# The first stage of a long convolution's transform, moved from the attention loop into the projection phase

## The chip, the cores and the metric

The kernel runs on one core of one Trainium2 chip, in one launch. A core has a matrix engine (PE, with its weight loads shown apart as PEld), a vector engine (DVE), an activation engine (ACT), a general engine (POOL) and a queue that issues the DMAs of this kernel (SP). The metric is the device time of one execution in microseconds; a kernel's time is the median of its runs.

## The reference: a state-space convolution beside multi-head attention

The output holds two results side by side, each 2048 rows of 448 columns. The left half is a long convolution of `u` with a kernel `K` that is a sum of 256 damped oscillations per column, done in the frequency domain at twice the length:

```python
def _A_ref(u, log_A_real, A_imag, C_real, C_imag, log_dt, D_skip):
    L = u.shape[1]
    dt = jnp.exp(log_dt)
    A = -jnp.exp(log_A_real) + 1j * A_imag
    C = (C_real + 1j * C_imag) * dt[:, None]
    P = jnp.exp((A * dt[:, None])[:, :, None] * pos[None, None, :])
    K = 2.0 * jnp.einsum("dn,dnl->dl", C, P).real
    Kf = jnp.fft.rfft(K, 2 * L)
    Uf = jnp.fft.rfft(u_t, 2 * L)
    y = jnp.fft.irfft(Uf * Kf[None, :, :], 2 * L)[:, :, :L]
    return y + u * D_skip[None, None, :]
```

The right half is softmax attention over 16 heads of 28 columns: `x @ wqkv`, scores times `28 ** -0.5`, softmax, times `v`, and the output projection `wo`. All numbers are float32.

## The kernel before, in words

**Projection phase.** The code from line 212 to line 551 computes q, k and v and the seeds of the convolution kernel. `work` (line 495) lists 48 projections (`qk_proj`, `v_proj`: twelve matmuls each) in four blocks of 512 rows of x; `transposes` (line 438) brings each block of x into the needed layout through the two PSUM banks `pt` (pool `ps_t`). Beside them run eight blocks of `seeds` (line 313), thirteen stages each, on DVE, ACT and POOL, which build the powers that the loop multiplies up. Both are laid out on 41 slots (line 530): in slot t the projections up to a share (t+1)/37 of the work are written, then the seed stages of that slot (stage i of block o in slot 4o + i, its load two slots ahead), then what `ahead[t]` holds, which are loads for the loop (from slot 26 on). In this phase instructions are not kept in the order in which they are written: a planner at build time orders them for each engine by its own estimates. The order on each engine and on SP's queue is then fixed. After slot 37 the tiles for the first units of attention are loaded (`khat`, `qhat`, `v`), and the maxima of unit 0 are computed.

**Attention loop.** From line 1006 a loop of 256 steps, written out, runs over 16 units (4 groups of heads by 4 blocks of queries) of 16 blocks of 128 keys. A step computes four score products `pss`, four products `pm` for the maxima of a later unit, four exponentials on ACT, and the eight passes of `po` that apply `p` to `v`. Here the order is that of the program on all engines (`KEPT["a"]`). Each step has two places `f` at which `slot` (line 957) puts one piece of side work: the building of the convolution kernel (`m_due`, 56 blocks, one every 3.5 steps, with its powers on DVE and POOL), then pieces of the transform of u (`u_due`), and late in the loop the spectrum and the final stage of the convolution.

**The transform of u** has two stages. The 2048 rows are seen as 32 by 64 (row = 64 n1 + n2). Stage 1 (`u_stage1`, line 567) takes, for four values of n2 in each of 16 rounds, sums over n1 with cosines and sines (`w1`, a block matrix of four 32 by 32 blocks); a round has one load step of four DMAs (each 32 partitions, rows of 112 elements), two parts (cosine, sine: one PSUM tile, four strips of matmul, one ACT copy into `ub`), and four DMAs that store to `yu_d`. Stage 2 (`u_stage2`, line 589) reads `yu_d` again, for two values of k1 in each of 16 rounds, with a matrix `mt` of its own (`m2u`), and leaves `uh_d` for the spectrum.

`u_due` (line 894) gives the step of each part: round i, part c at 3 + 3i + 1.5c, and 4 steps later for the rounds of stage 2, so that stage 1 runs over the steps 3 to 50 and stage 2 over the steps 55 to 104. The load of a round stands two rounds ahead. After the last part `load_wo` (line 704) clears and loads the output weights into the `ua` buffers of the same pool.

Of the kernel before, what the change touches and what calls it, by code (L numbers as in the profile page):

```python
# [8 lines left out]
F32 = mybir.dt.float32  # L9
F32R = mybir.dt.float32r  # L10
I32 = mybir.dt.int32
AF = mybir.ActivationFunctionType
# [6 lines left out]
D = 448  # L19
# [4 lines left out]
HG = H // G  # L24
CQ = 512
NQ = L // CQ
NK = L // 128
# [12 lines left out]
UG = (2, 2, 4)  # L40
PS = 1
SGB, XB, XL = 2, 5, 4
K0, KP, KD, UP = 0, 3.5, 4, 3
A0, A1, KW = 26, 34, (33, 35, 36)

N1 = 32
N2 = 64
CI = D // 4
# [42 lines left out]
def body(ctx, tc, a, out):  # L91
    nc = Engines(tc)
    nc.kept = KEPT["p"]
    x, wqkv, wo, u_a = a["B_x"][0], a["B_wqkv"], a["B_wo"], a["A_u"][0]
    out = out[0]
# [7 lines left out]
    dram = ctx.enter_context(tc.tile_pool(name="dram", bufs=1, space=DRAM))  # L103
# [1 line left out]
    kd_d = [dram.tile([2, 128, CQ], F32, name=f"kd_{g}") for g in range(G)]  # L105
    q_d = [[dram.tile([2, 128, CQ], F32, name=f"q_{g}_{c}") for c in range(NQ)] for g in range(G)]
    sd_d = [dram.tile([BO, 128, SDF], F32, name=f"sd_{o}") for o in range(NO)]
    yu_d = dram.tile([128, N1, D], F32, name="yu_d")
    uh_d = [dram.tile([128, N1 // 2, 2, DF], F32, name=f"uh_{f}") for f in range(2)]
    yk_d = [dram.tile([128, N1 // 4, NBF, 32], F32, name=f"yk_{f}") for f in range(2)]  # L110
    v_d = [dram.tile([128, G, NK // NQ, HG * 32], F32, name=f"v_{c}") for c in range(NQ)]
# [3 lines left out]
    const = pool(ctx, "const")  # L115
# [2 lines left out]
    sel = const.tile([128, HG], F32, name="sel")  # L118
    kones = const.tile([128, 1], F32, name="kones")
    w1 = const.tile([128, 2, 128], F32, name="w1")  # L120

    att, k0_st = ExitStack(), ExitStack()
    ps_w, n_ring = [None, 3], [0]

    def w_tile():

        n_ring[0] += 1
        return ps_w[0].tile([128, CQ], F32, name=f"pm{n_ring[0] % ps_w[1]}")

    q_p = pool(att, "q_p", side="right")  # L130
    v_p = pool(att, "v_p", side="right")
    kd_p = pool(att, "kd_p", side="right")
# [3 lines left out]
    def mm32(o, w, x_, start, stop, at=0):  # L136

        for i in range(w.shape[-1] // 32):
            c = slice(32 * i, 32 * i + 32)
            nc.tensor.matmul(o[c], w[:, c], x_, start=start, stop=stop, tile_position=(0, at + 32 * i))  # L140
# [4 lines left out]
    def load_k(g, j, p):  # L145
        if j == 0:
            t = k0_t if g == 0 else p.tile([128, HG, L], F32R, name="khat")
            kt_g[g] = [t[:, i] for i in range(HG)]
        for r in range(4):
            nc.sync.dma_start(kt_g[g][j][32 * r:32 * r + 32, :].bitcast(F32), k_d[g][r % 2, 32 * j:32 * j + 32, :])  # L150
# [61 lines left out]
    with ExitStack() as st:  # L212
# [6 lines left out]
        ps_t = pool(st, "ps_t", 2, PSUM)  # L219
# [40 lines left out]
        t = a["A_log_dt"]  # L260
# [7 lines left out]
        nc.gpsimd.memset(half_pi, TWO_PI / 4)  # L268
        nc.sync.dma_start(sel, a["sel"])
        nc.sync.dma_start(w1, a["w1"])  # L270
        for k in range(NCK):
            for s in (1, 0):
                src = wns[k][:, s, :].rearrange("p (g h e) -> p g h e", g=G, e=DH)
                hi, lo = (w_g[:, i, s, k, :, :, :DH] for i in range(2))
                nc.scalar.activation(hi, src, AF.Copy)
                nc.vector.tensor_tensor(lo, src, hi.bitcast(F32), ALU.subtract)
            nc.scalar.activation(vh[:, k, :], wns[k][:, 2, :], AF.Copy)
            nc.gpsimd.tensor_tensor(vl[:, k, :], wns[k][:, 2, :], vh[:, k, :].bitcast(F32), ALU.subtract)
# [201 lines left out]
        def v_proj(c, t):  # L480
# [11 lines left out]
                nc.sync.dma_start(v_d[c][:, :, t], vs.rearrange("p (g h) e -> p g (h e)", g=G))  # L492
            return evac

        work = []
        for c in range(NQ):
            jobs = [lambda c=c, s=s, g=g: qk_proj(c, s, g) for g in range(G) for s in (1, 0)]
# [15 lines left out]
        ahead = collections.defaultdict(list)  # L513
# [4 lines left out]

        for j, t in enumerate(KW):
            ahead[t].append(lambda j=j: load_k(0, j, k0_p))  # L520

        def project():

# [31 lines left out]
    kq_p = pool(kq_st, "kq_p")  # L555
# [8 lines left out]

    late = [False]

    def u_stage1(q):
        t_ = {}

        def load():  # L570
            u_in = t_["in"] = kq_p.tile([128, 8, CI], F32, name="ua", bufs=2)[:, :4]
            for j in range(4):
                nc.sync.dma_start(u_in[32 * j:32 * j + 32], bass.AP(
                    tensor=u_a.tensor, offset=u_a.offset + 4 * q * D + j * CI, ap=[[N2 * D, 32], [D, 4], [1, CI]]))

        def part(c):
            if c == 0:
                t_["out"] = kq_p.tile([128, 2, 4, CI], F32, name="ub", bufs=2)
            u_in, yt = t_["in"], t_["out"]
            pw = w_tile()  # L580
            mm32(pw[:, :D], w1[:, c, :], u_in.rearrange("p n i -> p (n i)"), start=True, stop=True)
            nc.scalar.activation(yt[:, c].rearrange("p n i -> p (n i)"), pw[:, :D], AF.Copy)
            if c == 1:
                for j in range(4):
                    nc.sync.dma_start(yu_d[8 * q:8 * q + 8, :, j * CI:(j + 1) * CI].rearrange("r k i -> k r i"),
                                      yt[32 * j:32 * j + 32].rearrange("p c n i -> p (c n) i"))
        return [load, lambda: part(0), lambda: part(1)]

    def u_stage2(m):
        t_ = {}  # L590

        def load():
            yu = kq_p.tile([128, 2, D], F32, name="ua", bufs=2)
            mt = kq_p.tile([128, 2, 128], F32, name="mt", bufs=2)
            t_["in"] = yu, mt
            nc.sync.dma_start(yu, yu_d[:, 2 * m:2 * m + 2, :])
            nc.sync.dma_start(mt, a["m2u"][:, 2 * m:2 * m + 2, :])

        def part(c):
            if c == 0:  # L600
                t_["out"] = kq_p.tile([128, 2, 2, DF], F32, name="ub", bufs=2)
            (yu, mt), us = t_["in"], t_["out"]
            pw = w_tile()
            for e in range(2):
                mm32(pw[64 * e:64 * e + 64, :D], mt[:, e, 64 * c:64 * c + 64], yu[:, e, :], True, True, 64 * e)
            for f in range(2):
                nc.scalar.activation(us[:, f, c, :].rearrange("p (b j i) -> p j b i", j=4, i=2),
                                     pw[:, f * DF:(f + 1) * DF].rearrange("p (j b i) -> p j b i", j=4, i=2), AF.Copy)
            if c == 1:
                for f in range(2):  # L610
                    nc.sync.dma_start(uh_d[f][:, m], us[:, f])
        return [load, lambda: part(0), lambda: part(1)]
# [260 lines left out]
    urgent, back = collections.deque(), collections.deque()  # L873
    powers = {"g": collections.deque(), "e": collections.deque()}
    done = {"mm": -1}
    u_jobs = [u_stage1(q) for q in range(16)] + [u_stage2(m) for m in range(16)]

    def u_load(i):
        if i < 32:
            u_jobs[i][0]()  # L880

    def u_part(i, c):
        u_jobs[i][1 + c]()
        if c and i not in (14, 15):
            u_load(i + 2)
        if c and i == 15:
            u_load(16)
            u_load(17)
        if c and i == 31:
            load_wo()  # L890

    u_load(0)
    u_load(1)
    u_due = collections.deque((3 + UP * i + (UP / 2) * c + (4 if i > 15 else 0), i, c) for i in range(32) for c in range(2))
    k_due = collections.deque(range(NB))
    m_due = collections.deque()

# [177 lines left out]
def constants():  # L1075
    import numpy as np
    k = {}
    k["ident"] = np.eye(128)
    sel, ones = np.zeros((128, HG)), np.zeros((128, 1))
    for j in range(HG):  # L1080
        sel[32 * j + DH, j] = 1.0
        ones[32 * j + DH:32 * j + DH + 2] = 1.0
    k["sel"], k["kones"] = sel, ones
    k["pw2"] = np.tile(2.0 ** np.arange(LV), (128, 1))
    n1, k1 = np.arange(N1), np.arange(N1)
    n2, k2 = np.arange(N2), np.arange(N2)
    th = 2 * np.pi * np.outer(n1, k1 + 0.25) / N1
    w1 = np.zeros((2, 128, 128))
    wb = np.zeros((2, 2, N1, 2, N1))
    for j in range(4):  # L1090
        w1[0, 32 * j:32 * j + 32, 32 * j:32 * j + 32] = np.cos(th)
        w1[1, 32 * j:32 * j + 32, 32 * j:32 * j + 32] = np.sin(th)
    for h in range(2):
        wb[h, 0, :, h, :] = np.cos(th).T / L
        wb[h, 1, :, h, :] = np.sin(th).T / L
    k["w1"] = w1.transpose(1, 0, 2)
    k["wb"] = wb.transpose(0, 1, 2, 4, 3).reshape(128, N2)
    ph = 2 * np.pi * ((k1[:, None, None] + 0.25) * n2[None, :, None] / L + n2[None, :, None] * k2[None, None, :] / N2)
    c, s = np.cos(ph).transpose(1, 0, 2), np.sin(ph).transpose(1, 0, 2)
    m2 = np.zeros((2, N2, N1, 2, 64))  # L1100
    m2[0, :, :, 0], m2[0, :, :, 1] = c, s
    m2[1, :, :, 0], m2[1, :, :, 1] = -s, c
    k["m2u"] = m2.reshape(2, 16, 4, N1, 128).transpose(1, 0, 2, 3, 4).reshape(128, N1, 128)
    wa = np.zeros((2, 64, N1, N2, 2))
    ct, st = c.transpose(2, 1, 0), s.transpose(2, 1, 0)
    wa[0, ..., 0], wa[0, ..., 1] = ct, -st
    wa[1, ..., 0], wa[1, ..., 1] = st, ct

    wa = wa.reshape(2, 64, N1, 2, 2, 16, 2).transpose(0, 1, 2, 5, 4, 3, 6)
    k["mw"] = np.concatenate([m2.reshape(128, N1, 128), wa.reshape(128, N1, 128)], -1)  # L1110
    return {n: v.astype(np.float32) for n, v in k.items()}
# [18 lines left out]
```

## Time and profile before

| | |
|---|---|
| median of three runs | 1304.48 us (1301.89 to 1305.05) |
| span of the profiled execution, first to last instruction | 1301.1 us |
| total of the profiled execution beyond its span | not given |
| instructions | 33177 |
| mean granted clock of PE | 0.978 |
| DMA moved | 205.35 MB, mean 158 GB/s |

The prediction sets its sum against the span and says how it stands to the median. In the rows, a group is named by engine, operation, output and input tiles; "x32" is the number of instructions. In the view by stretches, the columns are the stretch and its length, then busy time and instructions of each engine, then the clock that PE was granted, the busy share of the 16 DMA engines and what they moved. All instructions stand under line 75, a helper through which every operation goes; so they are told apart by the names of tiles.

### The profile page before, as it was taken

What the parts mean: (1) busy time and instruction counts of PE and PEld (TensorE: products, weight loads), DVE (VectorE), ACT (ScalarE), POOL (GpSimd) and SP (SyncE); (2) the same over time, 40 slices, a digit from 0 to 9 for tenths busy, and PEclk for the clock granted to TensorE, in tenths of its full rate; (3) what the DMA queues carried; (4) which work ended last, traced back from release to release, by engine and by line L of the source; (5) the groups of instructions that cost most, each with busy time, mean ns of one, the idle gap of its engine ahead of it and who ended that gap; (6) DMA issues with size and microseconds to landing.
All of it is one profiled execution on the core that took longest, in us unless ns stands there. A gap on an engine that the chain in (4) does not pass through costs nothing.

```text
span 1301.1 us, 33177 instructions
## 1 busy us (share of the span) xinstructions
PE 1228.2 (94%) x12625; PEld 701.0 (54%) x12625; DVE 948.0 (73%) x2106; ACT 952.4 (73%) x2068; POOL 871.1 (67%) x736
## 2 busy tenths in 40 slices
PE   6878985899999999999999999999999999999997
PEld 5657763355555555555555555555555555544433
DVE  5887896987777887787788888888888655645111
ACT  4775763488888888888888888888887766756552
POOL 3676683298888878888869999998996212424421
PEclk9888997999999999999999999999999999999999
DMA  6677769835866555458644131733425453647656
GB/s 194 203 258 244 249 206 294 237 77 124 195 137 149 124 146 148 140 147 231 181 126 96 54 95 32 182 91 83 103 51 148 153 158 133 201 144 244 198 162 174
DMA packets 200088, 205.35 MB, mean 158 GB/s; under 512 B 95993, under 2 KB 158521, under 8 KB 197881
## 3 DMA queue, kind: packets, MB, share of 16 engines
q1 hardware_dynamic: 199928, 203.23, 56.2%
q8 instruction: 100, 1.64, 0.5%
q14 instruction: 60, 0.48, 0.1%
HBM read 120.73 MB, written 82.18 MB: 156 GB/s over the span
## 4 chain that ended last, share of the span: by engine, by line
PE 71%; DVE 10%; DMA 6%; POOL 5%; ACT 3%; issue 3%; SPq 0%; POOLq 0%; ACTq 0%; DVEq 0%
PE pm L75 40%; PE pss L75 16%; PE po L75 15%; DVE tri L75 2%; DVE mx L75 2%; POOL e L75 1%; POOL qhat L75 1%; DMA k<-hl 1%; ACT tri L75 1%; DVE qhat L75 1%; DVE sg L75 1%; DMA tri<-in_B_wqkv 1%; DVE px L75 1%; DMA khat<-k 1%; DMA ut<-in_A_u 1%
## 5 line engine op out<-in xcount | busy, mean ns | idle before, releaser
L75 ACT ACTIVATE p<-pss 128x512 f32<-128x512 f32 x1024 | 560.9, 609 | 111.6 <-PE pss L75 108.6
L75 PE MATMUL pss<-qhat,khat 128*128 128x512 f32 x1024 | 402.5, 399 | 1.5 <-ACT p L75 1.4
L75 DVE TENSOR_REDUCE mx<-pm 128x1 f32<-128x512 f32 x500 | 321.4, 684 | 109.2 <-PE pm L75 107.1
L75 PE MATMUL pm<-khat,qhat 128*128 128x512 f32 x749 | 326.3, 438 | 3.4 <-DVE mx L75 2.1
L75 POOL TENSOR_TENSOR e<-e,sdb 128x256 f32<-128x256 f32 x168 | 202.0, 1202 | 116.2 <-ACT e L75 61.2
L75 PE MATMUL po<-p,v 128*32 128x512 f32 x2048 | 269.1, 594 | 0.0
L75 POOL TENSOR_TENSOR e<-e,eu 128x256 f32<-128x256 f32 x168 | 248.4, 1478 | 13.2
L75 PEld LDWEIGHTS pm<-khat,qhat 128*128 128x128 f32 x749 | 141.0, 189 | 199.7 <-ACT p L75 47.8
L75 DVE CUSTOM_DVE_ANT_0 rl<-pm,rl 128x512 f32<-128x512 f32 x249 | 171.4, 688 | 65.2 <-ACT rl L75 61.5
L75 PEld LDWEIGHTS pss<-qhat,khat 128*128 128x128 f32 x1024 | 190.2, 188 | 45.7 <-issue 10.8
L75 POOL TENSOR_TENSOR eu<-e,sdb 128x256 f32<-128x256 f32 x168 | 202.2, 1203 | 0.0
L75 POOL TENSOR_TENSOR p<-pr,pr 64x448 f32<-64x448 f32 x64 | 73.3, 1145 | 158.5 <-PE pm L75 133.2
L75 ACT ACTIVATE rl<-pm 128x512 f32<-128x512 f32 x249 | 150.8, 606 | 20.4 <-PE pm L75 20.4
L75 DVE TENSOR_TENSOR g<-g,zg 128x128 f32<-128x128 f32 x392 | 162.1, 413 | 3.4
L75 PE MATMUL pm<-xh,khat 112*128 112x512 f32 x256 | 94.1, 451 | 23.2 <-DVE hl L75 11.1
L75 PE MATMUL pm<-kdif,qhat 128*128 128x512 f32 x249 | 100.5, 404 | 2.6 <-DMA v<-v 1.3
L75 DVE TENSOR_TENSOR zg<-g,zg 128x128 f32<-128x128 f32 x224 | 88.0, 393 | 5.0
L75 PEld LDWEIGHTS pm<-e,g 128*32 128x32 f32 x3584 | 57.2, 109 | 43.8 <-issue 16.1
L75 DVE TENSOR_TENSOR pr<-pm,ub 128x448 f32<-128x448 f32 x64 | 37.0, 619 | 56.4 <-PE pm L75 42.0
L75 PEld LDWEIGHTS pm<-xh,khat 112*128 112x128 f32 x256 | 54.2, 217 | 39.4 <-DVE hl L75 12.9
L75 PE MATMUL pm<-e,g 128*32 128x64 f32 x3584 | 73.0, 222 | 1.9 <-POOL e L75 1.9
L75 ACT ACTIVATE y<-pm 128x448 f32<-128x448 f32 x48 | 26.5, 553 | 58.2 <-PE pm L75 33.8
(134 smaller groups left out, 1470.3 us busy)
## 6 DMA issues: line engine op xcount, KB each, us to landing
sdb<-sd SPq DMA_DIRECT2D x56, 336.0 KB
khat<-k SPq DMA_DIRECT2D x64, 256.0 KB
qhat<-q SPq DMA_DIRECT2D x64, 256.0 KB
sd<-sg SPq DMA_DIRECT2D x8, 1456.0 KB
k<-hl SPq DMA_DIRECT2D x16, 512.0 KB
q<-hl SPq DMA_DIRECT2D x16, 512.0 KB
mw<-in_mw SPq DMA_DIRECT2D x16, 512.0 KB
sd<-qhat SPq DMA_DIRECT2D x8, 896.0 KB
```

Source lines behind the costliest of these rows:

```text
L75: i = f(*args, **kw)
```

## The change

Stage 1 leaves the loop. Its 16 rounds stand in the slots `U1` of the projection phase, the load one slot ahead of the two parts. A round now takes the rows q, q + 16, q + 32, ... of u (128 of them, one on each partition, in full rows of 448), by one DMA; the block matrix is reordered to that (`wu`, a constant of its own beside `w1`, which other code still uses). Each part stores its 128 rows by one DMA. The tiles are borrowed: the input from the `v` buffers, the output from the `kdif` tiles, PSUM from `pt`. `yu_d` and the rows of `m2u` are reordered; stage 2 reads its input by two DMAs of 64 partitions in place of one. In the loop, `u_due` holds stage 2 alone, one round every 6 steps (`UP`) in place of 3, from step 3 on.

```diff
-K0, KP, KD, UP = 0, 3.5, 4, 3
+K0, KP, KD, UP = 0, 3.5, 4, 6
 A0, A1, KW = 26, 34, (33, 35, 36)
+U1 = (3, 4, 5, 6, 7, 8, 11, 12, 13, 14, 16, 17, 20, 21, 22, 23)
...
-    yu_d = dram.tile([128, N1, D], F32, name="yu_d")
+    yu_d = dram.tile([16, 4, N1, 2, D], F32, name="yu_d")
...
+    wu = const.tile([128, 2, 128], F32, name="wu")
...
+        nc.sync.dma_start(wu, a["wu"])
...
+        def u_stage1(q):
+            t_ = {}
+
+            def load():
+                t_["in"] = v_p.tile([128, NK // NQ, HG, 32], F32, name="v", bufs=5).rearrange("p t h e -> p (t h e)")[:, :D]
+                nc.sync.dma_start(t_["in"], u_a.rearrange("(p q) d -> q p d", q=16)[q])
+
+            def part(c):
+                ps = ps_t.tile([128, CQ], F32, name="pt")[:, :D]
+                mm32(ps, wu[:, c, :], t_["in"], True, True)
+                yt = kd_p.tile([128, CQ], F32R, name=f"kdif{2 * (q % 2) + c}").bitcast(F32)[:, :D]
+                nc.scalar.activation(yt, ps, AF.Copy)
+                nc.sync.dma_start(yu_d[q].rearrange("s k c d -> c (s k) d")[c], yt)
+            return load, lambda: part(0), lambda: part(1)
...
+        for q, t in enumerate(U1):
+            load, cos, sin = u_stage1(q)
+            ahead[t - 1].append(load)
+            ahead[t] += [cos, sin]
...
-    def u_stage1(q):
-        t_ = {}
-
-        def load():
-            u_in = t_["in"] = kq_p.tile([128, 8, CI], F32, name="ua", bufs=2)[:, :4]
-            for j in range(4):
-                nc.sync.dma_start(u_in[32 * j:32 * j + 32], bass.AP(
-                    tensor=u_a.tensor, offset=u_a.offset + 4 * q * D + j * CI, ap=[[N2 * D, 32], [D, 4], [1, CI]]))
-
-        def part(c):
-            if c == 0:
-                t_["out"] = kq_p.tile([128, 2, 4, CI], F32, name="ub", bufs=2)
-            u_in, yt = t_["in"], t_["out"]
-            pw = w_tile()
-            mm32(pw[:, :D], w1[:, c, :], u_in.rearrange("p n i -> p (n i)"), start=True, stop=True)
-            nc.scalar.activation(yt[:, c].rearrange("p n i -> p (n i)"), pw[:, :D], AF.Copy)
-            if c == 1:
-                for j in range(4):
-                    nc.sync.dma_start(yu_d[8 * q:8 * q + 8, :, j * CI:(j + 1) * CI].rearrange("r k i -> k r i"),
-                                      yt[32 * j:32 * j + 32].rearrange("p c n i -> p (c n) i"))
-        return [load, lambda: part(0), lambda: part(1)]
...
-            nc.sync.dma_start(yu, yu_d[:, 2 * m:2 * m + 2, :])
+            for c in range(2):
+                nc.sync.dma_start(yu[64 * c:64 * c + 64], yu_d.rearrange("q s k c d -> c (q s) k d")[c, :, 2 * m:2 * m + 2])
...
-    u_jobs = [u_stage1(q) for q in range(16)] + [u_stage2(m) for m in range(16)]
+    u_jobs = [u_stage2(m) for m in range(16)]
...
-        if c and i not in (14, 15):
+        if c:
             u_load(i + 2)
         if c and i == 15:
-            u_load(16)
-            u_load(17)
-        if c and i == 31:
             load_wo()
...
-    u_due = collections.deque((3 + UP * i + (UP / 2) * c + (4 if i > 15 else 0), i, c) for i in range(32) for c in range(2))
+    u_due = collections.deque((3 + UP * i + (UP / 2) * c, i, c) for i in range(16) for c in range(2))
...
+    wu = np.zeros((N1, 4, 2, 4, N1))
+    for j in range(4):
+        wu[:, j, 0, j], wu[:, j, 1, j] = np.cos(th), np.sin(th)
+    k["wu"] = wu.reshape(128, 2, 128)
...
-    k["m2u"] = m2.reshape(2, 16, 4, N1, 128).transpose(1, 0, 2, 3, 4).reshape(128, N1, 128)
+    k["m2u"] = m2.reshape(2, 4, 16, N1, 128).transpose(0, 2, 1, 3, 4).reshape(128, N1, 128)
```

More of the change, by code (lines that the diff above doesn't have):

```diff
@@ L875, in body @@
     done = {"mm": -1}
-    u_jobs = [u_stage1(q) for q in range(16)] + [u_stage2(m) for m in range(16)]
+    u_jobs = [u_stage2(m) for m in range(16)]
     def u_load(i):
-        if i < 32:
+        if i < 16:
             u_jobs[i][0]()
```

## The prediction, made before the changed kernel ran

> **What bounds the kernel now.** I read the page first: busy time, the 40 slices, the shares of the chain that ended last.
>
> ```profile
> PE 1228.2 (94%) x12625; PEld 701.0 (54%) x12625; DVE 948.0 (73%) x2106; ACT 952.4 (73%) x2068; POOL 871.1 (67%) x736
> ...
> PE   6878985899999999999999999999999999999997
> ...
> PEclk9888997999999999999999999999999999999999
> DMA  6677769835866555458644131733425453647656
> ...
> PE 71%; DVE 10%; DMA 6%; POOL 5%; ACT 3%; issue 3%; SPq 0%; POOLq 0%; ACTq 0%; DVEq 0%
> ```
>
> There are two regimes. For the first eight slices (about 254 us, the projection and the loads at its end) PE has gaps and a granted clock below full; from then on PE is at 9. The change takes work out of the second regime and puts it into the first, so I asked for busy times by stretch, and for the chain before 254 us alone.
>
> ```profile
> core 0: us, PE busy (x) PEld busy (x) DVE busy (x) ACT busy (x) POOL busy (x), PEclk, DMA share, GB/s
> 25.00:133.00 108.00, 88.50 (x386) 70.69 (x385) 88.22 (x155) 76.18 (x153) 69.67 (x77) 0.89 0.70 238
> 133.00:206.00 73.00, 60.27 (x263) 48.47 (x261) 59.74 (x101) 49.72 (x98) 55.36 (x61) 0.91 0.71 226
> 206.00:254.00 48.00, 32.27 (x78) 15.78 (x79) 39.15 (x87) 13.41 (x26) 2.43 (x4) 0.82 0.95 278
> 264.00:461.00 197.00, 196.42 (x2339) 107.28 (x2331) 154.07 (x365) 163.24 (x366) 163.33 (x129) 1.00 0.59 133
> 472.00:665.00 193.00, 192.07 (x2295) 104.68 (x2284) 149.60 (x354) 161.83 (x390) 151.17 (x119) 1.00 0.61 163
> 700.00:800.00 100.00, 99.73 (x1225) 57.22 (x1217) 87.45 (x208) 85.30 (x194) 96.63 (x79) 1.00 0.32 77
> ```
>
> ```profile
> by line: DVE tri L75 10.7%; PE pm L75 8.3%; POOL qhat L75 6.8%; DMA k<-hl 6.2%; issue 5.8%; ACT tri L75 5.1%; DVE qhat L75 5.0%; DVE sg L75 4.9%; DMA tri<-in_B_wqkv 4.2%; DVE px L75 4.2%; DMA khat<-k 3.9%; POOL tri L75 3.5%; DVE hl L75 3.1%
> ```
>
> In the loop PE is busy for 196.42 of 197 us: what leaves PE there shortens the run. Before it no engine rules: the chain hops between DVE, PE, POOL, ACT and DMA, the largest entry 10.7%, and each is 65 to 82% busy in 25 to 133 us. That is the dangerous kind of place: nothing is full, so added work is neither free nor fully paid.
>
> **What the loop gives back.** A part of stage 1 is one `u_stage1` call of `part(c)`: eight matmul passes and one ACT copy; there are 32, two in every three steps. Busy times of pipelined matmuls overlap, so I price a part by the pace of the steps. `fin` copies `po` once in 16 steps:
>
> ```profile
> 316.69 0.60 ACT L75 ACTIVATE o<-po 128x512 f32<-128x512 f32 x1
> 446.39 0.71 ACT L75 ACTIVATE o<-po 128x512 f32<-128x512 f32 x1
> ...
> 757.65 0.60 ACT L75 ACTIVATE o<-po 128x512 f32<-128x512 f32 x1
> ...
> 986.01 0.71 ACT L75 ACTIVATE o<-po 128x512 f32<-128x512 f32 x1
> ```
>
> The first pair is 32 steps with stage 1: 129.70/32 = 4.053 us. The second is 64 steps without any u: 228.36/64 = 3.568 us. The difference, 0.485 us a step, is 0.728 us a part (1.5 steps), against a mean of 0.94 us busy (30.1/32 from the row below). Stage 2 keeps its 32 parts, one every 3 steps instead of two: about 3.568 + 0.243 = 3.81 us a step up to step 99. So the loop gives 32 x 0.728 = **23.3 us**. The busy sum would say 30.1, but its excess is drain under the next matmul.
>
> Could another engine set the floor first? POOL is the next: 96.63 us in 100 us at the 3.568 us pace is 3.45 us a step, below 3.81. ACT and DVE have more room. The stall at the end of stage 2 stays: `load_wo` still clears two `ua` tiles on POOL behind the last stage-2 part.
>
> ```profile
> 664.24 0.85 POOL L75 MEMSET ua<- 128x896 f32 x1 [11.14 <-PE pm L75]
> ...
> PE pm L75 <- POOL e L75: 1.9, 2, 1.3
> ```
>
> POOL's 11.14 us there cost PE 1.9 us, in the chain; I keep that as it is (its change is worth 2 us either way at most).
>
> **What is moved to the projection.**
>
> ```profile
> L75 PE MATMUL pm<-ua,w 128*32 128x448 f32 x256 | 30.1, 541 | 0.0
> L75 ACT ACTIVATE ub<-pm 128x448 f32<-128x448 f32 x32 | 17.6, 550 | 19.6 <-PE pm L75 18.7 <-ACT ub L75 0.7
> ...
> L75 SPq DMA_DIRECT2D ua<-in_A_u x64: 311/430/1812, 250.6 to 434.3; - x64
> ...
> L75 SPq DMA_DIRECT2D yu_d<-ub x64: 302/450/1663, 273.8 to 461.1; - x64
> ...
> yu_d<-ub SPq DMA_DIRECT2D x64, 112.0 KB
> ...
> ua<-in_A_u SPq DMA_DIRECT2D x64, 56.0 KB
> ...
> L75 POOL TENSOR_TENSOR tri<-tr,pw x8: 2244/2249/3445, 31.1 to 181.4; 128x1232 f32<-128x1232 f32 x8
> ```
>
> The rounds stand in slots 3 to 23. The last row dates them: `phases` of seed block o stands in slot 4o + 4, so seven blocks, 28 slots, take 150.3 us, 5.37 us a slot; slot 3 is at about 26 us and the end of slot 23 near 138 us. The stretch of 25 to 133 us is theirs.
>
> *PE* gets the same 32 parts (the block matrix `wu` has the shape of `w1`), 23.3 us at full clock, on 88.50 busy of 108; idle are 19.5 there and 12.7 up to 206 us, 32.2 in all. *ACT* gets 17.6 us, 76.18 to 93.8 of 108. *DMA* gets (56 + 112) KB x 64 = 11.0 MB. At the 238 GB/s that 0.70 of the engines moved here (340 at a share of 1) that is 32 us of full DMA, 0.30 of the stretch: 0.70 becomes 1.00. In the loop the same bytes cost nothing, under a PE that is full at a share of 0.59. *SP* issues 16 loads and 32 stores and one constant (0.43 to 0.45 us each, about 22 us) and is spared 128 issues in the loop, where it gains 16 for the second halves of the stage-2 loads; those lie two rounds, 12 steps, ahead. The constant is 128 KB once. *Buffers*: the rounds borrow the `v` and `kdif` tiles, whose own loads come after slot 25; PSUM comes from the two `pt` banks that the transposes of x use.
>
> The DMA term can also be read by row length. 264 to 461 us, where these stores go out in rows of 448 B, gives 133/0.59 = 225 GB/s at a share of 1; the changed rows have 1792 B, like the longer rows of the projection at 340. The Trainium skill ("DMA: Bandwidth & Descriptors", section Specifications) asks for at least 512 B for full rate; these two rows agree. At 225 the 11.0 MB would be 49 us and the case below would lose 17 us more; at 340 it is the 32 us that I use.
>
> How much of this lengthens the projection? Waits of this stretch (PE's and ACT's, then the DMA queue's own):
>
> ```profile
> PE pm L75 <- DVE kb L75: 6.8, 4, 4.3
> PE pm L75 <- DVE hl L75: 6.8, 2, 5.4
> ...
> PE pt L75 <- DVE xl L75: 5.7, 3, 2.8
> ...
> ACT hl L75 <- DMA k<-hl: 3.2, 2, 2.3
> ACT vst L75 <- DMA v<-vst: 3.2, 2, 2.2
> ```
>
> ```profile
> SPq L75 <- POOL dhl L75: 33.9, 8, 8.4
> SPq L75 <- DVE hl L75: 13.5, 5, 4.9
> ```
>
> PE's gaps, 19.3 of 19.5 us, are waits for DVE to empty PSUM, in pieces of up to 5.4 us: an independent part placed there is free, one placed elsewhere pushes the next projection by 0.73 us. The order on PE is fixed at build time, so it can't choose at run time. From below the lengthening is -2 us: a warm PE can give back some of its 0.11 of lost clock on its 8.3% of 254 us of chain. From above it is 32 us, the DMA time with nothing hidden under it, the largest of the added loads. I take **12 us**, half of the PE time: PE would be asked for 88.50 x 0.89 + 23.3 = 102 of 108 us at full clock, too close to full for all to hide, while the gaps and the stretch up to 206 us hold more than 23.3. What is late next is the chain of seeds on ACT, through 32 copies of 0.55 us queued ahead of its own, then the loads before the loop.
>
> **Sum.** 1301.1 - 23.3 + 12 = 1289.8 us of span. The runs' median is 3.4 us over that profile's span (the profiled execution's own total isn't given; the fastest run lies 0.8 over it), so 1293 us. The bounds give 1301.1 + 3.4 - 23.3 - 2 = 1279 and 1304.5 - 23.3 + 32 = 1313.
>
> **Rivals.**
>
> *All of it hides, and the clock pays.* After an idle gap PE is slow:
>
> ```profile
> 83.00 2.08 PE L75 MATMUL pm<-xh,khat 112*128 112x512 f32 x4 [5.38 <-DVE hl L75]
> 84.87 0.63 PE L75 MATMUL pm<-xl,khat 112*128 112x512 f32 x1
> ...
> 89.89 0.63 PE L75 MATMUL pm<-xh,khat 112*128 112x512 f32 x2
> 90.36 0.40 PE L75 MATMUL pm<-xl,khat 112*128 112x512 f32 x1
> ```
>
> Four matmuls take 1.87 us from start to start (0.47 each) behind a gap of 5.38 us, and two 0.47 (0.235 each) some 5 us later. At a clock of 0.89 the 88.50 busy us hold 9.7 lost ones. u parts in the gaps would keep PE at 0.235; then the lengthening is 0 or a little less: 1281 us. For it: the idle 32.2 us exceed 23.3. Against it: the gaps of the waits above are few (nine), the parts 32. The Trainium skill ("TensorE: Matmul & The Clock Gate", Part 1) has the clock halve after an idle window of about 3.4 us; the rows above agree, and by that rule a part in each long gap speeds up what follows.
>
> *The projection takes it all back.* If the parts land between projections and not in gaps, each costs its 0.73 us again: 23.3 back, 1304 us. For it: the static order, and two `pt` banks that now serve parts and transposes in turn.
>
> *Slower: the DMA engines fill up.* Place: slots 3 to 23. The shares add to 1.00; the stretch from 206 us shows a share of 0.95, with PE busy for only 32.27 of 48 us. SP issues in order and stands up to 8.4 us for one `dhl`; a load of u queued there comes late, PE stands before its part, and `hl`, `vst` and `dhl`, with few buffers, stay taken by slow stores (the 3.2 us waits above grow). Price: up to the 32 us of DMA, less 23.3: +8.7, 1313 us. It decides once the stretch's share passes about 0.95 and its length 108 + 23 us. Against it: rounds leave out five of the 21 slots, and 133 to 206 us at 0.71 can take bytes that are late.
>
> *Not what it says*: the loop could keep its pace, if the 0.485 us a step came from ACT's or SP's share and not from PE. PE's 196.42 of 197 speaks against it; I give it no chance of its own.
>
> **How the numbers follow.** Half hidden (1285 to 1300) 0.45; all hidden 0.22; all taken back 0.17; DMA-bound 0.16. A measurement of this kernel can tell about 0.3%, 3.9 us, from no change, so the first two are faster (0.67), the third the same, the fourth slower. The range takes the bounds, 1279 to 1313.
>
> **What would show it.** The loop begins with the first `pss`:
>
> ```profile
> L75 PE MATMUL pss<-qhat,khat x1024: 387/396/505, 254.0 to 1275.7; 128*128 128x512 f32 x171
> ```
>
> Right: steps 16 to 48 of the loop at about 3.81 us (was 4.05) and a loop 23 us shorter from the first `pss` on; the first `pss`, now at 254.0 us, near 266; the stretch of 25 to 133 us stretched by some 10 us with PE's clock at or above 0.89 and a DMA share of 0.85 to 0.95. Wrong: a first `pss` after 277 us (taken back or worse; then the waits say whether for DMA or for PE), a step above 3.9 us (the pace wasn't PE's), or a gap in front of the u matmuls that a load ends.

## The result, and the profile after

Before: 1303.18 us median of 4 runs (1300.64 to 1305.05). After: 1309.63 us (1309.46 to 1311.34, 4 runs). The ratio is 1.0052, with a 95% interval of 1.0037 to 1.0067: half a per cent slower, where 1293 us had been forecast. The profiled execution of the changed kernel has a span of 1309.2 us (before 1301.1).

The first question is which half of the sum failed. Three groups of the changed kernel, by tile; the columns are the count, the shortest, median and longest duration in ns, then the first and last start in us:

```profile
L76 PE MATMUL pss<-qhat,khat x1024: 387/396/595, 284.4 to 1283.6; 128*128 128x512 f32 x171
...
L76 POOL TENSOR_TENSOR tri<-tr,pw x8: 2242/2248/2754, 31.5 to 204.0; 128x1232 f32<-128x1232 f32 x8
...
L76 ACT ACTIVATE hl<-pm x16: 577/594/637, 22.2 to 239.5; 128x512 fp32r<-128x512 f32 x16
```

The last of these groups in the kernel before:

```profile
L75 ACT ACTIVATE hl<-pm x16: 571/592/629, 21.8 to 210.1; 128x512 fp32r<-128x512 f32 x16
```

The loop begins at 284.4 us, **30.4 later** than before (254.0). From there to the end of the span it takes 1309.2 - 284.4 = 1024.8 us, **22.3 less** than before (1301.1 - 254.0 = 1047.1). The balance is the 8.1 us between the spans. The delay is there by the last copy of a projection (`hl<-pm`: 210.1 to 239.5, +29.4), and the stretch from it to the first `pss` is as long as it was (43.9 and 44.9 us). So it arose where the rounds were put; the seeds' `tri` lost 22.6 us of it (181.4 to 204.0).

The pace of the steps, by the copies that end steps 16, 32 and 64 of the changed kernel's loop (start, duration):

```profile
344.20 0.60 ACT L76 ACTIVATE o<-po 128x512 f32<-128x512 f32 x1
...
405.24 0.60 ACT L76 ACTIVATE o<-po 128x512 f32<-128x512 f32 x1 [0.17 <-PE po L76]
...
526.93 0.60 ACT L76 ACTIVATE o<-po 128x512 f32<-128x512 f32 x1 [0.16 <-PE po L76]
```

61.04/16 = 3.815 and 121.69/32 = 3.803 us a step, against a forecast of 3.81.

Now the projection. Busy times by stretch, from 25 us to the point some 4 us before the last `hl` copy, first in the kernel before, then in the changed one (columns as in the prediction):

```profile
25.00:206.10 181.10, 148.77 (x648) 119.16 (x646) 148.06 (x255) 125.90 (x249) 125.13 (x137) 0.90 0.70 233
```

```profile
25.00:235.40 210.40, 178.14 (x906) 123.75 (x904) 146.31 (x255) 143.75 (x283) 122.21 (x137) 0.92 0.76 253
```

PE is idle for 181.1 - 148.8 = 32.3 us of the first and for 210.4 - 178.1 = 32.3 us of the second. Its idle time, which was to take up half of the added matmuls, is as long as before; so PE's busy time and the stretch grew alike, by 29.4 and 29.3 us. What PE waits for (in total, times, longest), before and then after; `hl`, `kb`, `xl` and `vst` are tiles into which DVE or ACT copy results out of PSUM, `kdif` is the borrowed output tile:

```profile
PE pm L75 <- DVE hl L75: 13.2, 6, 5.4
PE pm L75 <- DVE kb L75: 6.8, 4, 4.3
PE pt L75 <- DVE xl L75: 6.1, 4, 2.8
```

```profile
PE pm L76 <- DVE kb L76: 8.2, 3, 5.1
PE pm L76 <- DVE hl L76: 7.3, 4, 3.9
PE pt L76 <- ACT kdif L76: 6.5, 3, 3.3
PE pt L76 <- DMA v<-in_A_u: 4.4, 1, 4.4
PE pt L76 <- DVE xl L76: 1.5, 2, 1.2
```

The waits for DVE did shrink, from 26.1 to 17.0 us. In their place stand two that the moved work brought with it: for the ACT copies of its own parts (6.5) and for a load of u (4.4). And parts do not stand only in gaps. The timeline of PE in the changed kernel, where two rounds run back to back with projections:

```profile
157.21 0.63 PE L76 MATMUL pm<-xh,khat 112*128 112x512 f32 x2
157.68 0.40 PE L76 MATMUL pm<-xl,khat 112*128 112x512 f32 x1
158.00 1.71 PE L76 MATMUL pt<-v,wu 128*32 128x448 f32 x16
159.64 0.73 PE L76 MATMUL pm<-xh,khat 112*128 112x512 f32 x2
...
162.31 0.40 PE L76 MATMUL pm<-xl,khat 112*128 112x512 f32 x1
162.64 1.71 PE L76 MATMUL pt<-v,wu 128*32 128x448 f32 x16
164.28 0.73 PE L76 MATMUL pm<-xh,khat 112*128 112x512 f32 x2
```

Sixteen matmuls, two parts, push the next projection by 1.64 us (158.00 to 159.64): 0.82 a part, against the 0.728 that a part cost in the loop. There nothing is hidden.

### The profile page after: what moved, and what is told of

Its sections match the earlier page's. It is cut to its first block, busy times and chain, and to the rows that moved or that the text cites. A ratio compares the mean times of both kernels' runs of the same rounds, so it can differ in the third digit from the quotient of the medians.

```text
span 1309.2 us, 33064 instructions
## 1 busy us (share of the span) xinstructions
PE 1235.3 (94%) x12625; PEld 696.8 (53%) x12625; DVE 944.4 (72%) x2106; ACT 954.0 (73%) x2070; POOL 866.6 (66%) x736
## 3 DMA queue, kind: packets, MB, share of 16 engines
q8 instruction: 100, 1.64, 0.5%
## 4 chain that ended last, share of the span: by engine, by line
PE 76%; DVE 11%; ACT 4%; POOL 3%; DMA 3%; issue 2%; SPq 0%; ACTq 0%; DVEq 0%; POOLq 0%
PE pm L76 42%; PE pss L76 17%; PE po L76 16%; DVE mx L76 2%; DVE tri L76 2%; ACT tri L76 1%; PE pt L76 1%; DVE px L76 1%; DVE rl L76 1%; DVE sg L76 1%; POOL qhat L76 1%; DMA khat<-k 1%; DVE qhat L76 1%; DVE hl L76 1%; DMA tri<-in_B_wqkv 1%
```

## The experiments

One number is read from each run, the start of the first `pss`; of the runs e1 to e18 each but e5 was executed once; the loop (span less that start) is the control, and it is 1023.8 to 1025.8 us in every run with all of stage 1 out of the loop and 1047.0 to 1050.4 in every run with all of it there. "New order" means the order that the planner makes for that kernel.

| run | what it is | first pss, us | span, us | time, us |
|---|---|---|---|---|
| before | | 254.0 | 1301.1 | 1303.18 |
| after | | 284.4 | 1309.2 | 1309.63 |
| e1_no_dma | moved matmuls and copies | 275.0 | 1299.6 | 1302.10 |
| e2_dma_only | moved loads and stores | 284.6 | 1308.4 | 1310.38 |
| e3_pe_only | moved matmuls | 269.0 | 1294.0 | 1296.15 |
| e4_pm_banks | after, parts in `pm` banks | 288.9 | 1314.7 | 1316.40 |
| e5_order_of_before | after, the rest in the order of before | 288.3 | 1313.2 | 1314.48 |
| e6_dma_only_order_of_before | e2, the rest in the order of before | 273.5 | 1297.4 | 1299.45 |
| e7_before_in_changed_order | before, projection in after's order | 276.6 | 1325.3 | 1327.42 |
| e8_before_in_dma_only_order | before, projection in e2's order | 285.7 | 1336.1 | 1338.20 |
| e9_before_pw38 | before, projections over 38 slots | 255.5 | 1302.6 | 1304.63 |
| e10_before_pw36 | before, projections over 36 slots | 265.0 | 1313.2 | 1315.33 |
| e11_rounds_slot_later | after, rounds one slot later | 287.8 | 1313.0 | 1314.80 |
| e12_changed_pw38 | after, projections over 38 slots | 288.2 | 1312.3 | 1314.46 |
| e13_new_layout_in_loop | before with the new rows | 263.2 | 1310.2 | 1312.15 |
| e14_half_of_the_rounds | 8 rounds moved | 272.8 | 1307.1 | 1308.83 |
| e15_pe_only_slot_later | e3, one slot later | 272.5 | 1297.4 | 1299.24 |
| e16_no_dma_slot_later | e1, one slot later | 275.1 | 1300.6 | 1302.75 |
| e17_loads_no_stores | after without the stores | 279.1 | 1304.0 | 1306.35 |
| e18_dma_only_slot_later | e2, one slot later | 288.4 | 1312.4 | 1314.66 |

The kernel before, run beside them, had medians of 1302.46 to 1304.87 us. Many starts fell outside the numbers of every theory that was set against them: by 1 us or less those of e1, e2, e5, e8, e11 and e18, by more those of e3, e4, e6, e10, e13 and e14.

**Parts of the moved work alone, and the banks.** The theory was that the two `pt` banks, shared with the transposes, cost most; the rivals were DMA and PE's own time. In e1 the rounds use one loaded tile and store nothing (stage 2 reads u itself); e3 leaves the copies out too; e2 has the DMAs without matmuls and copies.

In e1 and e3, then besides in e3 alone, then in e2, then in e4:

```diff
+                if q:
+                    t_["in"] = u_one[0]
+                    return
...
-                nc.sync.dma_start(yu_d[q].rearrange("s k c d -> c (s k) d")[c], yt)
```

```diff
-                nc.scalar.activation(yt, ps, AF.Copy)
```

```diff
-                mm32(ps, wu[:, c, :], t_["in"], True, True)
...
-                nc.scalar.activation(yt, ps, AF.Copy)
-                nc.sync.dma_start(yu_d[q].rearrange("s k c d -> c (s k) d")[c], yt)
+                nc.sync.dma_start(yu_d[q].rearrange("s k c d -> c (s k) d")[c], t_["in"])
```

```diff
-                ps = ps_t.tile([128, CQ], F32, name="pt")[:, :D]
+                ps = w_tile()[:, :D]
```

> The changed kernel without the DMAs of the moved stage: one load of u for all 16 rounds, no stores, and stage 2 of the loop reads u in place of the stage-1 result. PE parts and ACT copies stay. First pss was at 254.0 us before and at 284.4 us changed. Theory PE (the parts are paid whole, in a fixed order on PE): first pss at 276 to 284 us, at best the 4.4 us wait for a late load gone. Theory DMA (the 11.0 MB are the cost): first pss at 254 to 262 us.

> The changed kernel with the moved loads and stores alone: the loaded tile is stored twice as it is, no matmuls of stage 1, no ACT copies. Theory PE: first pss at 254 to 260 us. Theory DMA: 275 to 284 us.

> The changed kernel with the moved matmuls alone: one load of u, no ACT copies, no stores, stage 2 reads u. Theory PE: first pss at about 254 + 23 = 277 us. Theory evacuation (the parts hold the two pt banks until ACT has copied them, and the transposes of x wait): not above 265 us, as nothing holds the banks here.

> The changed kernel with the parts in the three pm banks of the projections in place of the two pt banks of the transposes. Theory evacuation: the 6.5 us that transposes wait for ACT's copy go, first pss at 276 to 279 us. Theory PE: within 3 us of 284.4, since another wait takes their place.

The bank theory found no support: in `pm` banks the wait for the copies of the parts all but went (0.2 us on `kdif`, 6.5 in the changed kernel), yet the start is 4.5 us later still. It is not excluded, because the planner's order of e4 has other costs: ACT runs 23 table loads (`ACT_TABLE_LOAD`, 1.28 us each) before the loop, against 17 in the changed kernel. Matmuls alone cost 15.0 us, with copies 21.0. DMA alone costs 30.6, as much as all of it. So the parts do not add up, and e2's waits do not name the DMA engines (waits of PE, e2):

```profile
PE pm L76 <- DVE hl L76: 24.1, 9, 8.2
PE pm L76 <- ACT vst L76: 8.9, 3, 6.0
PE pm L76 <- DVE kb L76: 7.5, 2, 4.1
```

**Is it the order?** Each of these kernels has other orders than before, not only for the moved instructions: on PE the first difference is instruction 85 of some 700 in the changed kernel. So I formed a second theory, that the added work is cheap and the broken order dear. The changed kernel and e2 got the instructions of before in the order of before on all five queues, by edges in the program (`PIN` lists the order of each queue), with only the moved ones free (e5, e6); and the kernel before got the projection order of the changed kernel and of e2 (e7, e8).

```diff
+        for n_, o_ in PIN.items():
+            l_ = nc.log[n_]
+            for i_, j_ in zip(o_, o_[1:]):
+                tc.add_manual_dep(l_[j_], l_[i_].name, mybir.DependencyInfo(
+                    mybir.DependencyClass.NoSync, mybir.DependencyReason.DATA), reason="order of before")
```

> The changed kernel, complete, with one thing fixed: on every engine and on SP's queue the instructions of the projection phase that the kernel before had too keep the order they had there; the planner may only place the moved ones among them. Theory order (adding the moved stage made the planner order the rest worse, and that is most of the cost): first pss at 260 to 275 us in place of 284.4, a span under 1300 us. Theory bytes (the 11.0 MB cost their time in any order): first pss at 280 to 288 us.

> The moved loads and stores alone (no stage-1 matmuls and copies; the loaded tile is stored as it is), the rest in the order of the kernel before. Theory order: first pss at 254 to 262 us, where the same work in the planner's own order had 284.6. Theory bytes: 278 to 288 us.

> The kernel before, with stage 1 in the loop and nothing of it in the projection phase; only the order of the projection phase's instructions, on all engines and SP, is that of the changed kernel. Theory order: first pss at 268 to 284 us with no added work at all. Theory bytes, and theory PE: 254 to 258 us.

> The kernel before, its projection phase in the order that the planner gave the run with the moved loads and stores alone (first pss 284.6 us there). Theory order: first pss at 272 to 285 us. Theory bytes: 254 to 258 us.

e7 and e8 looked like proof (22.6 and 31.7 us by order alone), but e5 contradicts them: with the order of before kept, the start is at 288.3 us, 3.9 later than with the new order (the time of e5 against the kernel before: ratio 1.0081, interval 1.0058 to 1.0105). PE's waits in e5:

```profile
PE pt L76 <- ACT kdif L76: 12.4, 6, 4.7
...
PE pt L76 <- DMA v<-in_A_u: 5.1, 1, 5.1
```

The two waits of the moved work are 17.5 us there, against 10.9 in the changed kernel. In e6 the planner, free only with the DMAs, set 18 of the 48 between 60 and 100 us. Its stretches, with the header of the view, and then its longest wait of ACT:

```profile
core 0: us, PE busy (x) PEld busy (x) DVE busy (x) ACT busy (x) POOL busy (x), PEclk, DMA share, GB/s
70.00:85.00 15.00, 14.40 (x75) 10.98 (x73) 13.23 (x28) 10.10 (x25) 12.61 (x18) 1.00 0.97 321
85.00:100.00 15.00, 1.29 (x4) 0.99 (x4) 4.11 (x6) 4.63 (x12) 4.64 (x2) 0.57 0.97 340
```

```profile
ACT hl L76 <- DMA k<-hl: 35.0, 5, 13.7
```

Here the DMA engines are full (0.97): the stores of the projections are issued among those of stage 1, ACT stands 13.7 us until a store frees an `hl` buffer, and PE does 1.29 us of work in 15. That is the slower rival of the prediction, in a kernel that is not the changed one.

Read in pairs of one order, the four runs say more. In the order of before the moved work costs 34.3 us (e5), its DMA alone 19.5 (e6), both with the load of `wu`. In the changed kernel's order the work costs 7.8 us (276.6 without it in e7, 284.4 with it). In e2's order the DMA costs nothing (285.7 without it in e8, 284.6 with it), so e2's 30.6 us are those of its order. A part of that order can be counted, the table loads of ACT up to 292 us in the kernel before, in the changed kernel and in e2 (busy time in total, mean ns of one, then the idle time before them):

```profile
L75 ACT ACT_TABLE_LOAD x15 | 19.2, 1283 | 1.0 <-PEq L1120 0.7
```

```profile
L76 ACT ACT_TABLE_LOAD x17 | 21.8, 1283 | 1.0 <-PEq L1123 0.7
```

```profile
L76 ACT ACT_TABLE_LOAD x25 | 32.1, 1283 | 1.1 <-PEq L1119 0.7
```

e8 has 25 as well; e5 and e6 have the 15 of the kernel before, e1 and e3 the 17 of the changed kernel.

**Neighbours.** An order made for other work says little about a kernel, so the next four runs let the planner make orders for the same work with its spacing changed a little.

```diff
-S0, SP, SW, SD, PW, E3 = 0, 4, 0, 5, 37, 8
+S0, SP, SW, SD, PW, E3 = 0, 4, 0, 5, 38, 8
...
-U1 = (3, 4, 5, 6, 7, 8, 11, 12, 13, 14, 16, 17, 20, 21, 22, 23)
+U1 = (4, 5, 6, 7, 8, 9, 12, 13, 14, 15, 17, 18, 21, 22, 23, 24)
```

> The kernel before with its 48 projections laid out over 38 slots instead of 37: no work is added or taken away, but the planner's orders change on every engine. Theory that the order of before is a lucky (tuned) one and that nearly any other costs some 20 us: first pss at 268 to 280 us (254.0 before), time 1318 to 1330. Rival, that the added work itself is what lengthens the projection and that orders without it are all much alike: first pss at 250 to 260 us, time 1300 to 1311.

> The kernel before with its 48 projections laid out over 36 slots: a second neighbour of its order. Same numbers as for 38 slots: 268 to 280 us (1318 to 1330) if the order of before is a lucky one; 250 to 260 us (1300 to 1311) if orders without the added work are alike.

> The changed kernel with every round of stage 1 one slot later (4 to 24): the same added work, another order. If the added work is the price, the first pss stays within 3 us of the 284.4 us of the changed kernel and the time at 1307 to 1313; if the order is, it moves by more than 6 us to either side (time below 1304 or above 1316).

> The changed kernel with its projections laid out over 38 slots, so that PE is asked for less per slot beside the rounds. If the price is the added work, the first pss stays within 4 us of 284.4 us; if the order decides, it moves by more than 6 us to either side; if it falls below 272 us the changed kernel only lacked its own spacing (time below 1298).

The start in a neighbour of before (e9), and in a neighbour of the changed kernel (e12):

```profile
L75 PE MATMUL pss<-qhat,khat x1024: 387/396/505, 255.5 to 1277.2; 128*128 128x512 f32 x171
```

```profile
L76 PE MATMUL pss<-qhat,khat x1024: 387/397/628, 288.2 to 1287.0; 128*128 128x512 f32 x171
```

The theory of a lucky order fell as the main cause: without the moved work the orders that the planner makes for that work start the loop at 254.0, 255.5 and 265.0 us, with it at 284.4, 287.8 and 288.2 (288.9 and 288.3 in e4 and e5). The two sets do not touch (e7 and e8, with orders made for other work, are left out). Among the orders made for the work of before the starts lie up to 11 us apart (e10); the moved work, with the order that the planner makes for it, is worth more. So a difference of a few us between two of these runs is no finding.

**Which of the moved work.** So the runs with matmuls alone and without DMA were repeated in another order, half of the rounds was moved, and the new layout was held apart.

In the loop's stage 1 of e13, then in e14:

```diff
-            for j in range(4):
-                nc.sync.dma_start(u_in[32 * j:32 * j + 32], bass.AP(
-                    tensor=u_a.tensor, offset=u_a.offset + 4 * q * D + j * CI, ap=[[N2 * D, 32], [D, 4], [1, CI]]))
+            nc.sync.dma_start(u_in.rearrange("p n i -> p (n i)"), u_a.rearrange("(p q) d -> q p d", q=16)[q])
```

```diff
+U1 = (3, 5, 7, 11, 13, 16, 20, 22)
...
+    u_jobs = [u_stage1l(q) for q in range(8, 16)] + [u_stage2(m) for m in range(16)]
```

> The kernel before with the new rows alone: stage 1 stays in the loop, one load and two stores a round, the reordered matrix (loaded at the start of the loop), two loads for a round of stage 2. If PE sets the loop's pace, as the prediction has it, 48 fewer loads and 96 fewer stores are worth nothing there: first pss at 254, time within 3 us of before. If the strided stores of before held the loop, 5 us or more are gained.

> Rounds 0 to 7 in the projection (slots 3, 5, 7, 11, 13, 16, 20, 22), rounds 8 to 15 in the loop in the new layout. If each round costs its share, the projection is 15 us longer (first pss near 269 us), the loop 11.6 us shorter, time near 1308. If a threshold decides (DMA engines full, or PE full), half of the rounds fits: first pss at 254 to 262 us, time 1291 to 1301. If any addition breaks up the order of before, first pss at 276 us or later, time 1315 or more.

> The run with the moved matmuls alone, every round one slot later: another order with the same work. If matmuls alone cost some 15 us whatever the order, first pss at 265 to 273 us; if that number was of one order, it moves by more than 6 us. This kernel leaves out the copies and stores of stage 1 and all of its loads but one; stage 2 reads u itself.

> The run with the moved matmuls and copies but one load and no store, every round one slot later. If the moved DMA costs some 9 us whatever the order, first pss at 273 to 281 us against 287.8 for the kernel with the same slots and its DMA; if the DMA is not what costs, 284 us or later. Leaves out all loads of stage 1 but one and all its stores; stage 2 reads u itself.

e13: in the loop the new rows are worth 0.1 us (1310.2 - 263.2 = 1047.0 against 1047.1), as a loop that PE paces should have it. But the start of the loop moved by 9.2 us, though no part stands in its projection. One thing is new there, the load of the matrix, written at the loop's start and issued by the planner at 18.3 us, long before its first use at 273.1 (e13, by tile):

```profile
L75 PE MATMUL pm<-ua,wu x256: 538/539/564, 273.1 to 468.0; 128*32 128x448 f32 x128
L75 SPq DMA_DIRECT2D wu<-in_wu x1: 431/431/431, 18.3 to 18.3; - x1
```

The stretch of its projection:

```profile
25.00:214.50 189.50, 152.02 (x649) 120.25 (x647) 148.83 (x255) 125.24 (x249) 125.09 (x138) 0.89 0.68 223
```

The order differs from that of before behind it (on ACT from instruction 25 on). Whether the 9.2 us are the order's or the load's own was not held apart; e10 shows that an order alone can be worth as much, and the traces lean that way: the fifth and the seventh `tri` multiplication of the seeds start at 123.7 and 161.0 us, against 123.6 and 160.7 before, and only the eighth is late (189.0 against 181.4). The changed kernel carries the same load (issued at 18.9 us).

From e13 on, matmuls alone add 5.8 us in one order and 9.3 in the other (269.0, 272.5), and here part of them is hidden (e3, by stretch):

```profile
25.00:220.30 195.30, 171.86 (x902) 120.34 (x900) 145.72 (x254) 129.33 (x251) 114.31 (x133) 0.94 0.66 219
```

PE is busy for 19.8 us more than in e13, and idle for 23.4 in place of 37.5. The copies add 6.0 and 2.6 us (275.0, 275.1); the DMA then adds 9.4 and 12.7 (284.4, 287.8). Half of the rounds costs 9.6 us over e13, where half of 21.2 is 10.6: near a share, and no sign of a threshold under which the rounds fit, though 9.6 us is also within what an order alone can be worth. Its loop gives 12.8, so e14 too stays slower than before (1308.83 against 1303.79).

**Loads, stores, and DMA alone again.** The edit of e17; e18 is e2 with the rounds one slot later.

```diff
-                nc.sync.dma_start(yu_d[q].rearrange("s k c d -> c (s k) d")[c], yt)
```

> The changed kernel, same slots, with all its loads of u but without the 32 stores; stage 2 reads u itself. The moved DMA cost 9.4 us here (275.0 without any, 284.4 with all). If its bytes are what costs, the loads are a third: first pss near 278 us. If the loads are what costs, because PE and SP wait for them, 283 us or later. If the stores are, because ACT waits for their buffers, 275 to 277 us. Leaves out the stores of stage 1.

> The moved loads and stores alone, every round one slot later. They cost 30.6 us in the planner's first order (first pss 284.6) and 19.5 in the order of before. If the DMA by itself costs some 11 us and the rest was the order, another order brings the first pss to 262 to 276 us; if DMA without matmuls really costs 30, it stays at 281 to 288 us. Leaves out the matmuls and copies of stage 1; the stores carry the loaded rows.

Loads add 4.1 of the 9.4 us with a third of the bytes; a difference of this size between two orders does not tell loads from stores. DMA alone is at 288.4 us again, not at 262 to 276. Its waits, in e18:

```profile
PE pm L76 <- DVE hl L76: 30.2, 11, 8.2
PE pm L76 <- ACT vst L76: 15.7, 4, 9.1
```

So in the planner's orders the moved DMA alone goes with all of the lengthening, and matmuls and copies beside it add nothing; taken the other way round, matmuls and copies cost 21.0 us and the DMA 9.4. But the two ways do not compare the same orders. e18 has the 25 table loads of e2 again, so it is no second opinion on that order, while e1, e16, the changed kernel and e11 all have 17; the pair of e8 and e2 gives the DMA nothing. The stretch of e2 shows what such an order does to PE:

```profile
25.00:235.90 210.90, 157.06 (x649) 123.71 (x647) 147.13 (x255) 139.50 (x259) 122.29 (x138) 0.84 0.77 253
```

PE is idle for 53.8 us there, and the matmuls of before hold it for 157.06 us in place of 148.77, at a granted clock of 0.84 in place of 0.90. ACT is busy for 139.50 us without any copy of stage 1, where it had 125.90 before. In the changed kernel PE is idle for 32.3 us at a clock of 0.92, as if the moved matmuls stood in what is empty here; but the two orders differ. Why the planner makes that order is open, and so is how much of the lengthening an order made by hand could save.

No run that does the whole computation beat the kernel before.

## Why the prediction was wrong, step by step

**The loop: right.** 23.3 us forecast, 22.3 measured, at 3.803 and 3.815 us a step against 3.81. POOL did not become the floor. That the 0.485 us a step was not the DMAs' is shown by e13: fewer and longer DMAs in the loop change nothing. ACT's share was not varied; PE's 196.31 us busy of 197 there speaks for PE.

**The lengthening of the projection, "I take 12 us, half of the PE time": the step that failed.** 30.4 us measured. The mechanism for PE itself held: matmuls alone cost 5.8 and 9.3 us over e13, and in e3 PE's idle time took up 14.1 of 19.8 us. What failed is that the 12 us stood for everything. The copies on ACT, the 11.0 MB of DMA, and the constant ("128 KB once") were named, and entered the sum at nothing; that the planner would order all the rest anew was not counted either. In the order in which the runs add them, they are worth 6.0, 9.4 and 9.2 us (the last is order or load, more likely order); with 5.8 for the matmuls that is the 30.4. These are differences of successive runs, which add up to the total whatever the cause, and each is within the 11 us that an order can be worth; so they are no exact prices. What holds beyond one order: without the DMA the loop starts at 275.0 and 275.1 us, with it at 284.4 and 287.8, with 17 table loads in all four; and in the order of before the DMA costs 19.5 us (e6, with the constant's load). By these the DMA's term of nothing was too small by some 10 to 20 us; only in e2's order, dear by itself (e8), did the DMA cost nothing. The start of five kernels with the moved work, 284.4 to 288.9 us, lies beyond that of the four without it, 254.0 to 265.0 us with e13. How much of the 30.4 is the work and how much the planner's new order stays open: in one order the whole work costs 34.3 us, in another 7.8.

**The gaps are not a store of free time.** That the gaps hold more than 23.3 us was true (32.3 us), and for the matmuls alone they did take some (14.1 us, e3). In the changed kernel PE was left with the same 32.3 us idle: the waits for copies and loads of the moved work came to 10.9 us, and those for DVE shrank by 9.1. The DMA estimate was sound as an amount: share times length is 0.70 x 181.1 = 127 us before and 0.76 x 210.4 = 160 after, 33 more against 32 forecast. Nearly the same number as the lengthening, but not because the engines were full: they stayed as free as before (54 and 50 us). The rounds were dated too early as well: expected at 26 to 138 us, their matmuls start from 41.6 to 171.9 us, and the share of 25 to 133 us, forecast at 0.85 to 0.95, was 0.75.

**The bounds: right.** -2 to 32 us holds 30.4, and 1279 to 1313 holds 1309.63. That the upper end came so near was luck: it is the time of the DMA at full engines, and they were not full.

**The rivals.** All hidden: fell; the granted clock hardly moved (0.90 to 0.92). All taken back, 1304 us: the sign of a first `pss` after 277 us came, but the lengthening passed 23.3. DMA-bound, 1313 us: its price of 32 us was near, its mechanism was not seen. It was to decide at a share of 0.95, and the share is 0.76; in stretches of 15 us the changed kernel reaches 0.90 at most, with PE busy throughout (100 to 115 us and 160 to 175 us). Only e6 shows the rival's chain of waits. So "slower" came true by a path that had no chance of its own: costs that the sum had at nothing, and a new order, added to the one that was counted. 0.16 was too little for that side.

**The rows of u.** The prediction read the DMA rate by row length. e13, where the loads and stores of stage 1 went from rows of 448 B to rows of 1792 B, shows it in the loop:

```profile
264.00:461.00 197.00, 196.31 (x2242) 106.40 (x2242) 155.01 (x368) 164.27 (x368) 166.66 (x132) 1.00 0.51 133
```

133 GB/s at a share of 0.51 is 261 at full, against 225 before. The Trainium skill ("DMA: Bandwidth & Descriptors", section Specifications) asks for rows of 512 B at least; the trace agrees, and no time came of it, since PE was full in both.

## What to carry to other kernels

In a phase where no engine rules and the chain hops between five of them, price each added instruction, DMA and constant at what it occupies, and let it be hidden only by a named gap that lasts until its own inputs and buffers are there; here PE's 32.3 us of idle time were as long after the change as before it. Where a planner makes the order, rerun the kernel of before with its spacing changed by a notch or two: that gives the spread which order alone is worth (up to 11 us here), and a run that pins another kernel's order does not (it gave 22.6 and 31.7 us). Such a run is of use against one with the same order and the work added. Test a suspected part both ways, alone and left out, and count what the planner did to the rest before believing either: the two gave 30.6 and 9.4 us for the same DMA, with ten more table loads on ACT than before in the first and two in the second.

## What had not been expected

One load of 128 KB, first used long after the projection, went along with a loop that begins 9.2 us later (e13). DMA alone, with no work for ACT, went along with 25 table loads on ACT in place of 15 (e2, e18). And 18 added DMAs of 224 KB within 40 us kept all 16 DMA engines at 0.97 over at least 30 us, and PE at 1.29 us of work in 15 with a granted clock of 0.57, in a phase whose mean share was 0.70 (e6).
